# Query features by products of 32 rows with repeated sketch rows, instead of outer products and transposes

## The chip, the cores and the metric

The kernel runs on one core of a Trainium2 chip. The metric is the device time of one execution in microseconds (us); less is better. The core has TensorE (matrix products, "PE" in the profile, with its weight loads listed apart as "PEld"), VectorE (DVE), ScalarE (ACT), GpSimd (POOL) and SyncE (SP), which here only issues transfers. Each engine works through its own list of instructions in order.

## What is computed

Polynomial-sketch attention, followed by a feed-forward layer with a squared ReLU. There are 4 batches with 4 heads of 1088 tokens, of 32 numbers each; the sketches S1 and S2 are 8 x 32; the feed-forward layer takes 4352 tokens of 128 numbers through 2048 and back.

```python
def phi(x):                                   # 32 numbers -> 64 features
    a = np.einsum('rd,bhsd->bhsr', S1, x)
    b = np.einsum('rd,bhsd->bhsr', S2, x)
    return np.einsum('bhsi,bhsj->bhsij', a, b).reshape(*x.shape[:-1], r * r)
q_p, k_p = (phi(q), phi(k))
kv = np.einsum('bhsf,bhsd->bhfd', k_p, v)
z = np.sum(k_p, axis=2)
num = np.einsum('bhsf,bhfd->bhsd', q_p, kv)
den = np.einsum('bhsf,bhf->bhs', q_p, z)[..., None] + 1e-06
x = (num / den), heads side by side           # 4352 x 128
h = np.maximum(x @ w_in, 0.0)
out = h * h @ w_out
```

All inputs and the output are float32.

## The kernel before

**Tiles.** Of each batch's 1088 tokens, 1024 are the main part; the other 64 ("remainder") go through the same steps in small tiles. The main part of a batch b is worked in two halves g, of 512 tokens and 4 heads each. Within a half there are four token tiles t of 128 tokens. The half's attention output, transposed (`xT`, 128 x 512, float16), is a *chunk* of the feed-forward layer. The first half of batch 0 is made in two chunks of 256 tokens, to start early; the remainders are a chunk of 256; that makes ten chunks.

**The feed-forward stream.** For every chunk, `block()` is called once for each of the 16 slices of 128 of the inner 2048 (once for two slices where a chunk has 256 tokens). It multiplies `xT` with a slice of `w_in` in float16 (L763, into `pg` in PSUM), ScalarE takes the ReLU (L770, `gt`), VectorE squares it (L771, `g2`), and TensorE multiplies the square with a slice of `w_o` in float32 (L790, accumulated in `po`). The first product runs about three blocks ahead of the second (`LOOK = 3`). The last chunk's second product has its operands swapped (L800). Results are transposed back (L709), scaled (L738) and stored.

**The attention work** for the next chunks is written as Python generators (`k_gen`, `phi_gen`, `x_gen`, `qrem_phi_gen` and others) that `pump` advances between blocks. A scheduler orders the instructions that this gives on each engine; only `start()`, which brings up the first chunks, is ordered by hand. A PSUM pool with the tag `ms` has two buffers of 128 x 512 float32; the transposes, the projections and the return transposes of the stores take turns on it.

**Features before.** A half of q is first laid out as `xt`, 128 x 512: partition 32 t + d holds number d of token tile t, and the 4 heads with 128 tokens each lie along the free axis. TensorE transposes do it (L235) for the halves (0,0), (0,1) and (3,1), a VectorE transpose of 32 x 32 blocks (L252) for the others. Then:

1. `projected` (L214): TensorE multiplies `xt` with the block matrix `w_bd` into `ab_ps` (128 tokens x 16 sketch values for each head and tile). These are small float32 products: for a half, 16 of them with 32 output rows and 64 columns each (at the start, 8 with 64 output rows). A float32 product is two records in the trace.
2. ScalarE copies `ab_ps` to `ab` (L63).
3. `outer_of` (L256): the 8 x 8 outer products, two instructions of 128 x 512 for a half, on GpSimd for the halves of batches 1 to 3, on VectorE for those of batch 0.
4. The features have to be turned to lie on the partitions, `phT`. For the halves (0,0), (0,1) and (1,0) TensorE transposes them (L437, L396, eight products of 128 x 128 each) and ScalarE copies the result (two copies of 512). For the other five halves `features_by_dma` has ScalarE split the words in 16-bit halves (L416, four copies of 512), stores them in DRAM (L422) and reads them back transposed by a DMA (L425).

With `phT` and the batch's `kvbd` (made from k and v, L318), `numerators` (L214, tile `nd`) gives the numerators and denominators; `normalize` (L478 to L517) divides and scales, and a transpose of `xs` gives `xT`.

k goes through steps 1 to 3 too, and needs no step 4.

Of the kernel before, what the change touches and what calls it, by code (L numbers as in the profile page):

```python
# [9 lines left out]
F16 = mybir.dt.float16  # L10
U16 = mybir.dt.uint16

# [10 lines left out]
def kernel(  # L23
# [29 lines left out]
    fpool = ctx.enter_context(tc.tile_pool(name="ffn", bufs=3))  # L53
    dram = ctx.enter_context(
        tc.tile_pool(name="dram", bufs=2, space=bass.MemoryType.DRAM)
    )
    pspool = ctx.enter_context(
# [119 lines left out]
    nc.scalar.activation(warm[:, 1:2], warm[:, 0:1], Relu)  # L177
    w_bd = cpool.tile([128, H * 16], F32)
    nc.vector.memset(w_bd[:], 0.0)
    kvbd = [cpool.tile([128, 4 * VW], F32, name=f"kvbd{i}") for i in range(2)]  # L180
# [81 lines left out]

    def proj(xt, T, tag, eng, outer, ps_tag="ms", m=32, only=None):

        return features(projected(xt, T, ps_tag, m), T, tag, eng, outer, only)

# [6 lines left out]

    def features(ab_ps, T, tag, eng, outer, only=None):
        ab = apool.tile([128, 256], F32, tag="ab", bufs=3)
        if T == 4:
            evict(
                eng,
                _v(ab, 0, [[16, 4], [64, 4], [1, 16]]),
                _v(ab_ps, 0, [[64, 4], [16, 4], [1, 16]]),  # L280
            )
        else:
            evict(eng, ab[:, 0:64], ab_ps[:, 0:64])
        ph = apool.tile([128, 1024], F32, tag=tag, bufs=3)
        for t0 in range(0, T, 2) if only is None else only:
            outer_of(ab, ph, t0, outer[(t0 // 2) % len(outer)], min(2, T - t0))
        return ph if only is None else (ab, ph)

# [115 lines left out]

    def features_by_dma(ph, eng):

        parted = apool.tile([128, 2048], U16, name="parted", tag="parted")  # L410
        halves = ph.bitcast(U16)

        for x in range(2):
            for y in range(2):
                with tc.issue_after(last_relu[0]):
                    eng.copy(  # L416
                        parted[:, 1024 * x + 512 * y : 1024 * x + 512 * y + 512],
                        _v(halves, 1024 * y + x, [[2, 512]]),
                    )
            yield 1  # L420
        rows_of = dram.tile([128, 2048], U16, name="rows_of", tag="rows_of")
        pinned(nc.sync.dma_start(rows_of[:, :], parted[:, :]))  # L422
        yield 2
        sb = apool.tile([128, 1024], F32, name="phT_d", tag="phT_d")
        pinned(nc.sync.dma_start_transpose(  # L425
            _v(sb.bitcast(U16), 0, [[256, 8], [1, 256]]),
            bass.AP(rows_of.tensor, rows_of.offset, [[1024, 256], [1, 1024]]),
        ))
        yield 4
        return sb  # L430

    def half_features_t(ph, t0, eng):

        t_ps = pspool.tile([128, 512], F32, name="t_ps", tag="ms", bufs=2)
        for pr in range(2):
            for t in range(2):
                nc.tensor.transpose(  # L437
                    t_ps[:, 256 * pr + 128 * t : 256 * pr + 128 * t + 128],
                    ph[:, 256 * (t0 + t) + 128 * pr : 256 * (t0 + t) + 128 * pr + 128],
                    iden[:, :],  # L440
                )
        sb = apool.tile([128, 512], F32, name="phT_h", tag=f"phT{t0 // 2}")
        evict(eng, sb[:, :], t_ps[:, :])
        return [sb[:, 256 * pr : 256 * pr + 256] for pr in range(2)]

    def numerators(b, phT, m, T=4, tag="nd", bufs=1):
        nd = pspool.tile([128, 256 * T], F32, name="nd", tag=tag, bufs=bufs)
        for t in range(T):
            for pr in range(2):
                both = not isinstance(phT, list)  # L450
                tiled(
                    nd, 256 * t + 2 * VW * pr, 2 * VW,
                    phT if both else phT[pr], 256 * t + 128 * pr if both else 128 * t,
                    kvbd[b % 2][:, 2 * VW * pr : 2 * VW * pr + 2 * VW],
                    m=m,
                )
        return nd
# [84 lines left out]
    summed = {0}  # L542
    ab_second = []
    BY_PE = ((0, 1), (B - 1, 1))
# [17 lines left out]
    def half_gen(phT, t0, m, tag, bufs):  # L562

        nd = numerators(0, phT, m, 2, tag, bufs)
        yield 1
# [21 lines left out]

    def phi_gen(b, g, outer):
        eng = nc.scalar
        xt = proj_t(q_sb[b], g, 4, eng) if (b, g) in BY_PE else turned(q_sb[b], g)  # L590
        yield 1
        ph = proj(xt, 4, "ph_q", eng, outer)
        if (b, g) == (1, 0):
            yield 3
            phT = []
            for pr in range(2):
                phT.append(feature_t(ph, 4, pr, eng))
                yield 1
            phT_of[b, g] = phT
            return  # L600
        yield 4
        phT_of[b, g] = yield from features_by_dma(ph, eng)

    def second_gen(outer, m):

        ph = features(ab_second[0], 4, "ph_q", nc.scalar, outer)
        yield 3
        phT = []
        for pr in range(2):
            phT.append(feature_t(ph, 4, pr, nc.scalar))  # L610
            yield 1
        yield from x_gen(0, 1, phT)
# [211 lines left out]
    def start():  # L824
# [3 lines left out]
        for h in range(H):  # L828
            nc.vector.tensor_copy(
                out=_v(w_bd, 16 * h, [[1, 16]], 32 * h, 32),  # L830
                in_=_v(s_ps, 0, [[1, 16]], 32 * h, 32),
            )
        xk.append(proj_t(k_sb[0], 1, 4, act))
        pk = [proj(x, 4, "ph_k", e, (dve,), "pg", m=64) for x, e in zip(xk, (dve, act))]
# [3 lines left out]
        kv0.tiles(pk[0], 0, range(2))  # L838
        pq = proj(xq, 4, "ph_q", act, (dve,), "pg", m=64, only=(0,))
        ph_krem[0] = proj(xkr, 1, "ph_kr", act, (dve,), "pg", m=64)  # L840
        outer_of(*pq, 2, dve)
        kv0.tiles(pk[0], 0, range(2, 4))
        kv0.tiles(pk[1], 1, range(4))
        pqT = [half_features_t(pq[1], 0, act)]
        kv0.finish((dve,))
        half = [half_gen(pqT[0], 0, 64, "pg", 2)]
        next(half[0])

# [7 lines left out]
        for _ in range(3):  # L856
            next(half[0])
        pqT.append(half_features_t(pq[1], 2, act))
        half.append(half_gen(pqT[1], 2, 64, "nd", 1))
        next(half[1])  # L860
# [4 lines left out]
        def rest():  # L865
            yield from half[1]
            yield from second_gen((dve,), 64)

# [5 lines left out]

        return rest(), last_casts(), xq

    second, last_casts, xq = start()
    by_hand.close()
    ab_second.append(projected(xq, 4, "ms", 64))

    for b in range(B):
# [8 lines left out]
        if b + 1 < B:  # L890
            add_work(
                phi_gen(b + 1, 0, (pool,)), phi_gen(b + 1, 1, (pool,)),
                after=7 if b == 0 else 1,
# [60 lines left out]
```

## Time and profile before

| | before |
|---|---|
| median of 3 runs | 208.66 us (208.07 to 208.98) |
| the profiled execution | 208.12 us |
| its span in the profile | 206.2 us |
| granted TensorE clock | 1.00 |
| TensorE busy | 196.8 us, 95% |
| weight loads | 120.1 us, 58% |
| VectorE busy | 146.7 us, 71% |
| ScalarE busy | 112.3 us, 54% |
| GpSimd busy | 45.5 us, 22% |
| outer products of 128 x 512 on GpSimd, half of them q's (L256) | 24, mean 1310 ns |
| the 16-bit copies (L416) | 20, mean 622 ns |
| squares (L771) | 136, mean 778 ns |

"Busy" is the time in which at least one instruction of the engine was running. TensorE's instructions overlap each other, so that a record's own duration is longer than the time by which it holds up the next one; the distance from start to start is what counts. The chain of waits follows the last instruction back to what released it, step by step.

### The profile page before, as it was taken

The page shows a single profiled execution, that of the slowest core. Times are in us where ns is not written, and L with a number is a line of the kernel's source. Part 1 is how long each engine was busy: PE and PEld are TensorE (multiplying, and loading weights), DVE is VectorE, ACT ScalarE, POOL GpSimd, SP SyncE. Part 2 cuts the span into 40 slices and gives each one's busy share as a digit, 9 for nine tenths or more (in the row PEclk, how much of TensorE's full clock was granted, in tenths as well). Part 3 has the DMA queues.
Part 4 walks back from the last instruction along what each step waited for, and adds up shares of the span by engine and source line. Part 5 has one row for each costly group of instructions (what it writes and reads, how often), then busy time and mean ns, then how long its engine had stood idle before and what let it go on. Part 6 is the DMA issues. An engine that isn't in the chain of part 4 may idle for free.

```text
span 206.2 us, 5349 instructions
## 1 busy us (share of the span) xinstructions
PE 196.8 (95%) x2177; PEld 120.1 (58%) x2177; DVE 146.7 (71%) x281; ACT 112.3 (54%) x216; POOL 45.5 (22%) x66
## 2 busy tenths in 40 slices
PE   7979999698999999999999999999999999999993
PEld 6857888474434543554344645455444454779992
DVE  2769769539786799869966896569666887766651
ACT  3548765208755448336755365547755545655540
POOL 1000539242100097105400295114000210000000
PEclk9999999999999999999999999999999999999999
DMA  6899301412468124651260022401440101010001
GB/s 167 218 327 320 70 3 53 111 30 32 116 191 191 30 38 115 136 153 27 61 187 8 17 67 105 102 3 37 150 93 3 51 0 25 5 51 13 16 0 51
DMA packets 40120, 17.39 MB, mean 84 GB/s; under 512 B 27040, under 2 KB 39072, under 8 KB 40096
## 3 DMA queue, kind: packets, MB, share of 16 engines
q1 hardware_dynamic: 40016, 17.05, 31.5%
q8 instruction: 17, 0.28, 0.5%
q14 instruction: 7, 0.06, 0.1%
q10 hardware_dynamic: 80, 0.01, 0.0%
HBM read 8.79 MB, written 4.85 MB: 66 GB/s over the span
## 4 chain that ended last, share of the span: by engine, by line
PE 75%; DVE 9%; POOL 4%; DMA 3%; ACT 3%; issue 3%; SPq 1%; DVEq 0%; ACTq 0%
PE po L790 40%; PE pg L763 12%; PE po L800 7%; POOL ph L256 4%; PE nd L214 4%; PE ab_ps L214 3%; DVE g L771 3%; PE xt_ps L235 2%; DMA t<-in_q_dram 2%; PE kv_first L193 1%; DMA rows_of<-parted 1%; PE kv_ps L318 1%; ACT gt L770 1%; SPq L425 1%; PE kv_first L318 1%
## 5 line engine op out<-in xcount | busy, mean ns | idle before, releaser
L771 DVE TENSOR_TENSOR g<-gt 128x512 f32<-128x512 f32 x136 | 104.0, 778 | 36.9 <-ACT gt L770 36.6
L790 PE MATMUL po<-g,w_o 128*128 128x512 f32 (+1 forms) x288 | 123.8, 526 | 0.4
L770 ACT ACTIVATE gt<-pg 128x512 f32<-128x512 f32 x136 | 81.0, 600 | 50.0 <-PE pg L763 49.0
L790 PEld LDWEIGHTS po<-g,w_o 128*128 128x128 f32 x288 | 52.5, 191 | 26.4 <-issue 12.3
L763 PE MATMUL pg<-xT,w_in 128*128 128x512 f16 x112 | 42.6, 381 | 0.5 <-ACT gt L770 0.4
L256 POOL TENSOR_TENSOR ph<-ab 128x512 f32<-128x512 f32 (+1 forms) x27 | 33.1, 1250 | 17.9 <-ACT ab L63 17.7
L763 PEld LDWEIGHTS <-w_in 128*128 128x128 f16 x160 | 15.3, 98 | 22.3 <-issue 18.7
L514 POOL TENSOR_SCALAR mp<-mm 128x4 f32<-128x4 f32 (+2 forms) x11 | 4.0, 364 | 96.6 <-DVE mm L494 96.6
L800 PEld LDWEIGHTS po<-w_o,g 128*128 128x128 f32 x128 | 16.4, 192 | 0.6
L800 PE MATMUL po<-w_o,g 128*128 128x128 f32 x128 | 16.5, 275 | 0.0
L63 ACT COPY ab<-ab_ps 128x256 f32<-128x256 f32 (+1 forms) x19 | 6.4, 341 | 16.6 <-PE ab_ps L214 16.5
L214 PEld LDWEIGHTS ab_ps<-w_bd,xt 128*32 128x32 f32 (+1 forms) x476 | 8.7, 113 | 7.8 <-ACT gt L770 2.3
L416 ACT COPY parted<-ph 128x512 uint16<-128x512 uint16 x20 | 11.6, 622 | 1.1 <-POOL ph L256 1.1
L214 PE MATMUL ab_ps<-w_bd,xt 128*32 128x64 f32 (+1 forms) x476 | 11.6, 223 | 0.2
L252 DVE STREAM_TRANSPOSE xt<-t 128x512 f32<-128x512 f32 x9 | 6.1, 696 | 3.0 <-DMA t<-in_q_dram 3.0
L63 ACT COPY xt<-xt_ps 128x512 f32<-128x512 f32 (+1 forms) x11 | 5.1, 471 | 4.5 <-PE xt_ps L235 4.4
L318 PEld LDWEIGHTS kv_ps<-v_main,ph 128*32 128x32 f32 x384 | 4.1, 110 | 6.0 <-issue 4.3
L318 PE MATMUL kv_ps<-v_main,ph 128*32 128x33 f32 x384 | 4.9, 198 | 2.0 <-DVE xs L508 1.4
L214 PEld LDWEIGHTS nd<-kvbd,phT_d 128*32 128x32 f32 x320 | 4.9, 110 | 3.2 <-issue 1.7
L63 ACT COPY sb<-t_ps 128x512 f32<-128x512 f32 (+1 forms) x8 | 3.4, 429 | 5.0 <-PE t_ps L396 4.9
L508 DVE TENSOR_TENSOR xs<-nd,small 128x512 f16<-128x512 f32 (+1 forms) x9 | 5.7, 632 | 0.3
L763 PE MATMUL pg<-xT_h,w_in 128*128 128x256 f16 x32 | 5.8, 273 | 0.0
(74 smaller groups left out, 118.1 us busy)
## 6 DMA issues: line engine op xcount, KB each, us to landing
rows_of<-parted SPq DMA_DIRECT2D x5, 512.0 KB, 2.8
t<-in_k_dram SPq DMA_DIRECT2D x3, 512.0 KB, 4.2
t<-in_q_dram SPq DMA_DIRECT2D x3, 512.0 KB, 4.2
out_dram<-o_sb SPq DMA_DIRECT2D x20, 64.0 KB, 1.8
w_in<-in_moe_w_in_dram SPq DMA_DIRECT2D x2, 512.0 KB, 7.6
w_o<-in_moe_w_out_dram SPq DMA_DIRECT2D x2, 512.0 KB, 8.5
v_turned<-in_v_dram SPq DMA_DIRECT2D x64, 16.0 KB, 2.0
k_sb<-in_k_dram SPq DMA_DIRECT2D x2, 256.0 KB, 3.0
```

The costliest lines, as they stand in the source:

```text
L63: return nc.scalar.copy(dst, src)
L214: nc.tensor.matmul(out_ps[p0 + c : p0 + c + m, c0 : c0 + w], lhsT[:, l0 + c : l0 + c + m], rhs,)
L252: nc.vector.transpose(out=xt[:, :], in_=_v(src, 128 * g, [[NJ * D, 4], [1, 128]]))
L256: eng.tensor_tensor(out=_v(ph, 256 * t0, [[64, 4 * w], [8, 8], [1, 8]]), in0=_v(ab, 64 * t0, [[16, 4 * w], [1, 8], [0, 8]]), in1=_v(ab, 64 ...
L318: nc.tensor.matmul(self.ps[c : c + self.m, at : at + w], _v(ph, c0 + 128 * pr + c, [[1, self.m]], p0, n), v_of(2 * pr + c // 64), start=c ...
L416: eng.copy(parted[:, 1024 * x + 512 * y : 1024 * x + 512 * y + 512], _v(halves, 1024 * y + x, [[2, 512]]),)
L508: nc.vector.tensor_tensor(out=_v(xs, 0, [[128, T], [32, 4], [1, 32]]), in0=num, in1=_v(rs, 0, [[4, T], [1, 4], [0, 32]]), op=mult,)
L763: nc.tensor.matmul(pg[:, nt * i : nt * i + nt], w_in[:, 128 * (c + i) : 128 * (c + i) + 128], xT[:, 0:nt],)
L770: last_relu[0] = nc.scalar.activation(gt[:, :], pg[:, :], Relu).ins
L771: nc.vector.tensor_tensor(out=g2[:, :], in0=gt[:, :], in1=gt[:, :], op=mult)
L790: last_product[0] = nc.tensor.matmul(po[0][:, 0:nt], w_o[:, 128 * c : 128 * c + 128], g2[:, nt * i : nt * i + nt], start=(c == 0), stop=(c ...
L800: nc.tensor.matmul(po[t // 2][:, 128 * (t % 2) : 128 * (t % 2) + 128], g2[:, 128 * t : 128 * t + 128], w_o[:, 128 * c : 128 * c + 128], st ...
```

## The change

Features of q are made in their final layout at once. In `start()`, two copies make `w_rep`, 128 x 128: on each group of 32 partitions, the columns 0 to 63 are the rows of S1, each repeated 8 times in a row, and the columns 64 to 127 the rows of S2, all 8 repeated 8 times over. `features_direct` then multiplies, for a token tile t, its 32 partitions of `w_rep` with its 32 partitions of `xt`: 64 features come out on 64 partitions, for two heads side by side (c = 0, 1), once for the factor a and once for the factor b. ScalarE copies the a part from PSUM (`a_rep`), and VectorE multiplies it with the b part, straight into `phT`.

A half takes two calls of `features_direct`, with two tiles t each. A call has 8 float32 products with 32 contraction rows, 64 output rows and 256 columns, 2 copies of 128 x 256 and 2 multiplications of 128 x 256. It takes both buffers of the tag `ms`, one for each t. Gone for q's main halves are `projected`, its copy, the outer products, the transposes of features, the 16-bit copies and the ten transfers through DRAM. k and the remainders keep the old way. In the changed program the halves (2,0) and (3,0) have their first call taken apart by the scheduler: the four products of one t, a first product of the feed-forward stream, then the four of the other t.

```diff
+    w_rep = cpool.tile([128, 128], F32)
...
-    def features_by_dma(ph, eng):
...
-        for x in range(2):
-            for y in range(2):
-                with tc.issue_after(last_relu[0]):
-                    eng.copy(
-                        parted[:, 1024 * x + 512 * y : 1024 * x + 512 * y + 512],
-                        _v(halves, 1024 * y + x, [[2, 512]]),
+    def features_direct(xt, ts, phT):
+        f = {t: pspool.tile([128, 512], F32, name="f_ps", tag="ms", bufs=2) for t in ts}
+        for ab in range(2):
+            for t in ts:
+                for c in range(2):
+                    nc.tensor.matmul(
+                        f[t][64 * c : 64 * c + 64, 256 * ab : 256 * ab + 256],
+                        w_rep[32 * t : 32 * t + 32, 64 * ab : 64 * ab + 64],
+                        _v(xt, 128 * c, [[256, 2], [1, 128]], 32 * t, 32),
                     )
...
-        pinned(nc.sync.dma_start(rows_of[:, :], parted[:, :]))
...
-        pinned(nc.sync.dma_start_transpose(
...
+        a = apool.tile([128, 512], F32, name="a_rep", tag="a_rep", bufs=3)
+        for i, t in enumerate(ts):
+            nc.scalar.copy(a[:, 256 * i : 256 * i + 256], f[t][:, 0:256])
+        for i, t in enumerate(ts):
+            nc.vector.tensor_tensor(
+                out=phT[:, 256 * t : 256 * t + 256],
+                in0=a[:, 256 * i : 256 * i + 256], in1=f[t][:, 256:512], op=mult,
+            )
...
-    def phi_gen(b, g, outer):
+    def phi_gen(b, g):
         eng = nc.scalar
         xt = proj_t(q_sb[b], g, 4, eng) if (b, g) in BY_PE else turned(q_sb[b], g)
         yield 1
-        ph = proj(xt, 4, "ph_q", eng, outer)
...
+        phT = phT_tile()
+        for x in range(2):
+            features_direct(xt, (2 * x, 2 * x + 1), phT)
+            yield 1
+        phT_of[b, g] = phT
...
+        nc.vector.tensor_copy(
+            out=_v(w_rep, 0, [[8, 8], [1, 8]]), in_=_v(s_ps, 0, [[1, 8], [0, 8]])
+        )
+        nc.vector.tensor_copy(
+            out=_v(w_rep, 64, [[8, 8], [1, 8]]), in_=_v(s_ps, 8, [[0, 8], [1, 8]])
+        )
...
         kv0.tiles(pk[0], 0, range(2))
-        pq = proj(xq, 4, "ph_q", act, (dve,), "pg", m=64, only=(0,))
         ph_krem[0] = proj(xkr, 1, "ph_kr", act, (dve,), "pg", m=64)
-        outer_of(*pq, 2, dve)
         kv0.tiles(pk[0], 0, range(2, 4))
+        phT = phT_tile()
+        features_direct(xq, (0, 1), phT)
         kv0.tiles(pk[1], 1, range(4))
-        pqT = [half_features_t(pq[1], 0, act)]
         kv0.finish((dve,))
-        half = [half_gen(pqT[0], 0, 64, "pg", 2)]
+        features_direct(xq, (2, 3), phT)
+        half = [half_gen(phT, 0, 64, "pg", 2)]
```

## The prediction

> **What bounds the kernel.** I read the engines' shares first, then the chain of waits, then TensorE's order of time, then its idle time by stage.
>
> ```profile
> PE 196.8 (95%) x2177; PEld 120.1 (58%) x2177; DVE 146.7 (71%) x281; ACT 112.3 (54%) x216; POOL 45.5 (22%) x66
> ```
>
> A busy share alone proves nothing, since records overlap. The chain of waits, in a stretch without attention work, does:
>
> ```profile
> 63.45 0.22 PE pg L763
> 63.67 0.86 PE po L790 x2
> 64.53 0.22 PE pg L763
> 64.75 0.86 PE po L790 x2
> ...
> 192.42 0.89 PE po L800 x8
> ```
>
> A block lasts 1.08 us, and all of it is TensorE: 0.22 for one float16 product of 512 columns and 0.86 for one float32 product, two records of 0.43. In the same block ScalarE works 0.60 and VectorE 0.69, so both have slack. The price goes with the columns: a record of 512 columns takes 0.43, one of 128 columns 0.89/8 = 0.11 us. A record of 256 columns thus takes 0.215.
>
> Where attention work is put between blocks, it lengthens TensorE's list (order of time):
>
> ```profile
> 115.87 0.60 PE L709 MATMUL o_ps<-iden,oT 128*128 128x128 f32 x4
> ...
> 116.40 0.65 PE L214 MATMUL ab_ps<-w_bd,xt 128*32 128x64 f32 x32
> ...
> 116.99 0.39 PE L763 MATMUL pg<-xT,w_in 128*128 128x512 f16 x1
> ```
>
> The projection of a half, 32 records, holds TensorE from 116.40 to 116.99, 0.59 us. A record of 64 columns should take 0.055; 32 one after another would take 1.8. So four run side by side, each on 32 output columns of the array: 8 x 0.055 = 0.45. The remaining 0.14, and 0.09 more by which the four transposes before took longer than 4 x 0.11, is the change to narrow products and back. I call that 0.24 us for a group.
>
> The stages show how much waiting there is to win (columns are the stage, its length, then each engine's busy time):
>
> ```profile
> 2.00:17.00 15.00, 13.53 (x207) 10.96 (x208) 8.96 (x31) 7.53 (x17) 0.85 (x4) 1.00 0.98 281
> 17.00:30.00 13.00, 12.91 (x143) 10.60 (x140) 9.96 (x16) 10.05 (x22) 3.74 (x5) 1.00 0.43 112
> 30.00:50.00 20.00, 17.43 (x408) 12.96 (x406) 13.15 (x28) 7.96 (x17) 9.56 (x12) 1.00 0.25 57
> 68.00:100.00 32.00, 31.59 (x487) 15.49 (x486) 27.27 (x52) 17.01 (x35) 14.34 (x17) 1.00 0.35 79
> 113.00:136.00 23.00, 22.91 (x431) 12.32 (x433) 16.19 (x27) 12.73 (x27) 9.44 (x9) 1.00 0.24 65
> ```
>
> TensorE idles 2.6 us at 30 to 50 and hardly anywhere after it. Distances from start to start, against the prices above, add a little: 3.3 us of waits at 30 to 50, 1.4 at 68 to 100, 0.5 at 17 to 30, 1.7 at the start.
>
> **Removed from TensorE.** I count seven halves, all but (0,0), which is at the start. Each loses a projection, 0.45 + 0.24 = 0.69: 4.8 us. Halves (0,1) and (1,0) lose 8 transposes each: 16 x 0.11 = 1.8. Sum 6.6. The other five halves were transposed by DMA, off TensorE, so nothing else comes back there.
>
> **Added to TensorE.** A call of `features_direct` is 8 products, 16 records of 256 columns, each on 32 rows and 64 columns of the array. Four different tiles follow each other (two t, two c). No row shows products side by side on different rows. Bounds: four side by side, as the projection has it by columns, 16 x 0.215/4 = 0.86; two by two, 1.72; one by one, 3.44. With 0.24 that is 1.10, 1.96 or 3.68. I take 1.10: the projection is the nearest row, and each t has its own PSUM buffer. 14 calls make 15.4 us. In the changed program's order two calls stand in two halves, one t each; a half has two tiles only and lasts 8 x 0.215/2 + 0.24 = 1.10, so each costs a call more: 2.2. Five calls have a third product of the first t ahead of the second t's, on a tile in use: 0 to 2 records each, I take one, 0.2: 1.0. Sum 18.6, net +12.0 us.
>
> The Trainium skill ("TensorE: Matmul & The Clock Gate", Part 3, "Measured speedup vs the span model") reports 3.07 times, not 4, for four products of 32 rows side by side. An estimate by it makes a call 16 x 0.215/3.07 + 0.24 = 1.36, and the sum 16 x 0.26 = 4.2 us higher.
>
> **The start.** There the chain decides. Before, the first half's normalization begins at 13.07 on VectorE; its four small transposes and copy (10.82 to 12.1) go. In their place two calls stand among the k products, and the second call's two multiplications stand ahead of that normalization on VectorE. They wait for a call that ends near 12.6, so it begins near 13.7: +0.6 us (0 to 1.5). Two copies for `w_rep` (near 0.3 each, like the 0.295 us copy of `kvbd`) fall where VectorE waits for `ab_ps`.
>
> **The other engines.**
>
> ```profile
> L256 POOL TENSOR_TENSOR ph<-ab 128x512 f32<-128x512 f32 x24 | 30.8, 1310 | 11.9 <-ACT ab L63 11.7
> ...
> L416 ACT COPY parted<-ph 128x512 uint16<-128x512 uint16 x20 | 11.6, 622 | 1.1 <-POOL ph L256 1.1
> ...
> L63 ACT COPY ab<-ab_ps 128x256 f32<-128x256 f32 x15 | 5.6, 373 | 15.1 <-PE ab_ps L214 15.1
> ...
> L738 DVE TENSOR_TENSOR o_sb<-o_ps,beta 128x256 f32<-128x256 f32 x2 | 0.8, 410 | 0.0
> ```
>
> These are groups of instructions (busy time, mean ns of one, idle time before). The single line on the squares adds least, median and longest:
>
> ```profile
> L771 DVE TENSOR_TENSOR g<-gt x136: 627/693/1551, 17.1 to 199.7; 128x512 f32<-128x512 f32 x136
> ```
>
> VectorE gains 32 multiplications, priced by the 410 ns row: +13.1, and loses four outer products of 0.69: -2.7. Squares have a median of 693 but a mean of 778 ns, and the long ones lie beside GpSimd's outer products (at 118 to 122 us one of 1.10 and two that make 2.64). Half of those outer products go, so perhaps half of 136 x 0.085 = 11.6 us. VectorE ends near 151 us: not a bound. ScalarE loses 20 x 0.62, 8 x 0.37 and six copies of 0.58, and gains 32 x 0.37: about -7 us, hidden. GpSimd loses 12 x 1.31. The ten DRAM transfers free SP's queue, where the load of q at 86.9 stands behind one of them; TensorE is full there.
>
> **Waits.** *Won:* at 36 us TensorE waits 1.4 us for k's products, as GpSimd has a queue of six outer products, and again 0.6 at 40.7. Only k's stay, so I take 2.4 of the 3.3 us there, and 0.6 of the 1.4 at 68 to 100, where squares come late beside GpSimd: -3.0 (0 to -6.9, with all waits listed). *New:* a call holds both `ms` buffers until VectorE has multiplied. A second call follows a block later, 1.08 us; copy, multiplication, and a ReLU or square in front of each take up to 0.37 + 0.41 + 0.60 + 0.69 = 2.1. Behind it on TensorE the next block's products are queued. Bounds 0 and 14 x 1.2 = 17. The copy of a needs the first half of a call only, and existing waits of this kind are under 0.8, so I take near the lower end, 0.27 for each of seven second calls: +1.9.
>
> Sum: 12.0 + 0.6 - 3.0 + 1.9 = +11.5 us on the profiled 208.12 (span 206.2 and 1.9 around it). The median is 0.54 higher: 208.66 + 11.5 = 220.2 us.
>
> **Rivals.** *Two by two:* the rows of the array do not run side by side. A call takes 1.96: 14 x 1.96 + 2 x 0.24 - 6.6 = +21.3; the start +2, waits -3 + 1: 230.0 us. For: no row shows it otherwise. Against: nothing in the column case hints at it. The Trainium skill (same page and part, "The mechanism") says that a weight load overlaps a running product only where their row groups differ. By that rule c = 0 and c = 1 of one t would follow each other, which gives this rival's time. The trace disagrees for columns: the projection's loads all use 128 rows, and 32 of them fit in its 0.59 us.
>
> *The buffers:* waits for `ms` reach 1.0 us a call, 14 us instead of 1.9: 232 us. For: VectorE's list mixes normalization (3 us for a half) with the multiplications. Against: where VectorE is as full before, at 68 to 100 us, TensorE still waits only 1.4 us.
>
> *Faster:* the columns of a 32-row product stream twice as fast, the two records of a product running together. A call is 0.43 + 0.24 = 0.67, sixteen (with split ones) 10.7 - 6.6 = 4.1, and all 6.9 us of waits go, with 0.3 at the start: 206.2 us. It decides from a call below 0.82 us, with all waits won. Against: at 128 rows a column costs the same for 128, 256 and 512 columns, and the waits would all have to go at once.
>
> **Numbers.** My forecast 0.67, two by two 0.16, the buffers 0.08, faster 0.06, one by one 0.03 (14 x 1.72 above two by two, 254 us). My forecast's own range, from its bounds, is 213.5 to 226 us. To hold 8 in 10 the range takes in two by two: 212.5 to 231.5. About 0.5% is what a measurement of this kernel can tell from no change. Faster by more 0.06, within it 0.02, slower 0.92.
>
> **What would show it.** Groups of 16 records of `f_ps`, 1.1 us from the first start to the next product; starts four together, 0.215 apart. TensorE at 95% or more, its list 12 us longer, GpSimd near 25 us, ScalarE near 105. No gap at 36 us. The forecast is wrong if a call takes 1.9 us, if TensorE stands idle before `f_ps` for over 5 us in all, or if the span is under 211.

## The result, and the profile after

The changed kernel takes 225.46 us (median of 6 runs, 225.2 to 226.9), the kernel before beside it 208.82: a ratio of 1.0805, with a 95% interval of 1.0763 to 1.0847. A second series of the same two kernels gave 1.0691 (1.0638 to 1.0745). The forecast was 220.2 us, slower by 11.5; measured were 16.6 and, in the second series, 14.4 (0.0691 x 207.81). That second ratio rests on two of its four runs (222.15 and 222.78 us); the other two (226.31 and 226.49 us, at mean clocks of 0.977 and 0.976) lie over 1.5% above them and are left out, although two runs of the first series took as long at the same clocks (225.88 and 226.9 us).

The engines' shares of the changed kernel, from its page:

```profile
PE 213.4 (96%) x2185; PEld 126.3 (57%) x2185; DVE 145.8 (65%) x311; ACT 108.9 (49%) x214; POOL 28.0 (13%) x54
```

TensorE is the bound as before, with 16.6 us more of busy time. VectorE, ScalarE and GpSimd have less to do. The groups (busy time, mean ns of one, idle time before):

```profile
L743 DVE TENSOR_TENSOR g<-gt 128x512 f32<-128x512 f32 x136 | 94.7, 702 | 37.9 <-ACT gt L742 36.1
...
L421 DVE TENSOR_TENSOR phT_q<-a_rep,f_ps 128x256 f32<-128x256 f32 x32 | 12.5, 418 | 16.7 <-ACT a_rep L419 16.7
L412 PE MATMUL f_ps<-xt,w_rep 32*64 32x256 f32 x256 | 23.0, 388 | 0.0
L419 ACT COPY a_rep<-f_ps 128x256 f32<-128x256 f32 x32 | 11.1, 374 | 20.0 <-PE f_ps L412 19.8
L254 POOL TENSOR_TENSOR ph<-ab 128x512 f32<-128x512 f32 (+1 forms) x15 | 15.1, 1024 | 37.2 <-ACT ab L59 37.2
```

The new multiplications cost VectorE 12.5 us. They are paid for by four outer products that go (2.7 us) and by the squares, whose mean falls from 778 to 702 ns. In the profile before, the 20 squares that overlap an outer product of GpSimd last 1.27 us on average and the others 0.69; after, 9 overlap one, and they last 0.74, which the smaller number of outer products alone does not explain. L412 is what TensorE got for it: 256 records.

The timeline shows how long a call of `features_direct` holds TensorE (start, duration, count; in brackets the idle time before and its releaser):

```profile
27.42 1.09 PE L412 MATMUL f_ps<-xt,w_rep 32*64 32x256 f32 x16
28.44 0.39 PE L735 MATMUL pg<-xT_h,w_in 128*128 128x256 f16 x2
...
80.35 1.08 PE L412 MATMUL f_ps<-xt,w_rep 32*64 32x256 f32 x8
81.36 1.12 PE L762 MATMUL po<-g,w_o 128*128 128x512 f32 x2
...
82.42 0.65 PE L212 MATMUL ab_ps<-w_bd,xt 128*32 128x64 f32 x32
...
83.00 1.70 PE L412 MATMUL f_ps<-xt,w_rep 32*64 32x256 f32 x16
...
83.19 0.37 ACT L59 COPY ab<-ab_ps 128x256 f32<-128x256 f32 x1 [1.34 <-PE ab_ps L212]
...
84.63 0.39 PE L735 MATMUL pg<-xT,w_in 128*128 128x512 f16 x1
```

A whole call lasts 1.02 us from its start to the next product (27.42 to 28.44), its 16 records in four groups of four. Half a call, with one t, lasts 1.01 (80.35 to 81.36): with two tiles of the array instead of four, half the work takes the same time. The call at 83.00 takes 1.63: one of the two `ms` buffers still holds the `ab_ps` of 82.42, which ScalarE copies until 83.56, so one t goes two by two first and the other follows. Five of the whole calls are of this kind. All calls together hold TensorE 21.8 us.

Two stretches hold what the forecast did not have. The first is the start, in stages (length, busy time of PE, PEld, DVE, ACT, POOL, granted clock, DMA share, GB/s):

```profile
13.00:17.00 4.00, 3.32 (x74) 2.38 (x70) 2.41 (x9) 1.80 (x5) 0.00 (x0) 1.00 1.09 367
17.00:23.00 6.00, 4.26 (x19) 3.15 (x20) 5.48 (x16) 3.54 (x7) 2.71 (x7) 0.72 0.90 229
```

```profile
18.10 0.28 PE L513 MATMUL x_ps<-iden,xs 128*128 128x128 f16 x2 [1.48 <-DVE xs L489]
...
20.93 2.54 PE L762 MATMUL po<-g,w_o 128*128 128x256 f32 x6
```

TensorE waits for `xs`, the granted clock falls to a mean of 0.72, and six records of 256 columns take 2.54 us, against 1.56 in e12, where the clock stays at 1.00. The second is the load of q for batch 2. SP's own queue, before and then after:

```profile
33.55 0.36 SPq L746 DMA_DIRECT2D out_dram<-o_sb  x1
...
53.42 0.39 SPq L83 DMA_DIRECT2D t<-in_q_dram  x1
```

```profile
42.23 0.37 SPq L718 DMA_DIRECT2D out_dram<-o_sb  x1
42.69 1.18 SPq L79 DMA_DIRECT2D t<-in_k_dram  x1
43.93 16.95 SPq L110 DMA_DIRECT2D v_turned<-in_v_dram  x32
60.98 0.39 SPq L79 DMA_DIRECT2D t<-in_q_dram  x1
```

and what comes of it on TensorE and VectorE:

```profile
41.21 0.38 PE L681 MATMUL o_ps<-iden,oT 128*128 128x128 f32 x2
...
64.31 0.38 PE L735 MATMUL pg<-xT,w_in 128*128 128x512 f16 x1
65.11 0.71 DVE L250 STREAM_TRANSPOSE xt<-t 128x512 f32<-128x512 f32 x1 [3.62 <-DMA t<-in_q_dram]
65.74 0.65 DVE L743 TENSOR_TENSOR g<-gt 128x512 f32<-128x512 f32 x1
...
66.45 1.12 PE L762 MATMUL po<-g,w_o 128*128 128x512 f32 x2 [1.76 <-DVE g L743]
```

The order on SP is that of before: the first output store, then k, 32 transfers of v, then q. But the store needs the return transposes `o_ps`, which take turns on `ms`, and these now stand behind the calls of (0,1) and (1,0) on TensorE's list. They start at 41.21 instead of 31.85 us, the store at 42.23 instead of 33.55, and q's load at 60.98 instead of 53.42. A transpose of that q stands ahead of a square on VectorE, so VectorE waits 3.62 us (1.32 before) and TensorE waits for the square, which it did not before.

By chunks (the start of each chunk's first product with `w_o`, before and after, in these two profiles) the 17.2 us by which the span grew come as follows: the start +3.1, chunk 0 to 1 +5.2, 1 to 2 -2.5, 2 to 3 +1.7 (the late q), 3 to 4 +5.0, 4 to 5 -0.3, 5 to 6 +5.1, and -0.1 in all that follows.

### The profile page after: what moved, and what is told of

It is laid out like the page before. It is cut to its first block, busy times and chain, and to the rows that moved or that the text cites. A ratio compares the mean times of both kernels' runs of the same rounds, so it can differ in the third digit from the quotient of the medians.

```text
span 223.4 us, 5360 instructions
## 1 busy us (share of the span) xinstructions
PE 213.4 (96%) x2185; PEld 126.3 (57%) x2185; DVE 145.8 (65%) x311; ACT 108.9 (49%) x214; POOL 28.0 (13%) x54
## 4 chain that ended last, share of the span: by engine, by line
PE 88%; DMA 6%; DVE 3%; ACT 1%; issue 0%; SPq 0%; DVEq 0%; ACTq 0%
PE po L762 44%; PE pg L735 14%; PE f_ps L412 10%; PE po L772 6%; PE nd L212 4%; DMA t<-in_q_dram 4%; PE ab_ps L212 3%; PE xt_ps L233 3%; PE kv_ps L316 2%; DMA k_sb<-in_k_dram 2%; PE o_ps L681 1%; PE kv_first L316 1%; DVE xt L250 1%; ACT xt L59 1%; DVE phT_q L421 1%; DVE g L743 1%
## 5 line engine op out<-in xcount | busy, mean ns | idle before, releaser
L743 DVE TENSOR_TENSOR g<-gt 128x512 f32<-128x512 f32 x136 | 94.7, 702 | 37.9 <-ACT gt L742 36.1
L421 DVE TENSOR_TENSOR phT_q<-a_rep,f_ps 128x256 f32<-128x256 f32 x32 | 12.5, 418 | 16.7 <-ACT a_rep L419 16.7
L412 PE MATMUL f_ps<-xt,w_rep 32*64 32x256 f32 x256 | 23.0, 388 | 0.0
L419 ACT COPY a_rep<-f_ps 128x256 f32<-128x256 f32 x32 | 11.1, 374 | 20.0 <-PE f_ps L412 19.8
L254 POOL TENSOR_TENSOR ph<-ab 128x512 f32<-128x512 f32 (+1 forms) x15 | 15.1, 1024 | 37.2 <-ACT ab L59 37.2
L412 PEld LDWEIGHTS f_ps<-xt,w_rep 32*64 32x64 f32 x256 | 11.7, 131 | 7.5 <-DVE phT_q L421 2.2
L212 PEld LDWEIGHTS nd<-kvbd,phT_q 128*32 128x32 f32 (+1 forms) x480 | 8.0, 111 | 5.3 <-PE pg L735 2.6
L212 PE MATMUL nd<-kvbd,phT_q 128*32 128x66 f32 (+1 forms) x480 | 9.4, 222 | 0.3 <-DVE phT_q L421 0.3
L212 PEld LDWEIGHTS ab_ps<-w_bd,xt 128*32 128x32 f32 (+1 forms) x252 | 5.4, 124 | 5.6 <-ACT gt L742 1.5
L212 PE MATMUL ab_ps<-w_bd,xt 128*32 128x64 f32 (+1 forms) x252 | 7.2, 235 | 0.1
```

The lines of the kernel that those rows point to most:

```text
L212: nc.tensor.matmul(out_ps[p0 + c : p0 + c + m, c0 : c0 + w], lhsT[:, l0 + c : l0 + c + m], rhs,)
L254: eng.tensor_tensor(out=_v(ph, 256 * t0, [[64, 4 * w], [8, 8], [1, 8]]), in0=_v(ab, 64 * t0, [[16, 4 * w], [1, 8], [0, 8]]), in1=_v(ab, 64 ...
L412: nc.tensor.matmul(f[t][64 * c : 64 * c + 64, 256 * ab : 256 * ab + 256], w_rep[32 * t : 32 * t + 32, 64 * ab : 64 * ab + 64], _v(xt, 128 ...
L419: nc.scalar.copy(a[:, 256 * i : 256 * i + 256], f[t][:, 0:256])
L421: nc.vector.tensor_tensor(out=phT[:, 256 * t : 256 * t + 256], in0=a[:, 256 * i : 256 * i + 256], in1=f[t][:, 256:512], op=mult,)
L743: nc.vector.tensor_tensor(out=g2[:, :], in0=gt[:, :], in1=gt[:, :], op=mult)
```

## The experiments

Lines of their code have other numbers than in the kernels shown. "Edit" is against the changed kernel unless said otherwise.

**e1: the start as before.** Edit: `start()` makes the half (0,0) with outer products and transposes again.

```diff
+        pq = proj(xq, 4, "ph_q", act, (dve,), "pg", m=64, only=(0,))
...
+        outer_of(*pq, 2, dve)
...
-        features_direct(xq, (0, 1), phT)
...
+        pqT = [half_features_t(pq[1], 0, act)]
...
-        features_direct(xq, (2, 3), phT)
```

> The changed kernel, but the first half (0,0) in start() is made the old way (projection, outer products on VectorE, eight TensorE transposes); all other halves stay with features_direct. Theory 'the start': the first block came 3.0 us later, and TensorE's long wait before it (1.65 us at 16.4) brings down its clock, so that records of 0.216 take 0.43 us until 22.9; both go. Expected 225.5 - 3.0 - 1.5 = 221.0 us. Rival 'the start is cheap': it costs 0.6 us as predicted and the rest of the 3.0 us is k's transfer, which landed 0.75 us later in that one execution: 224.9 us, with the clock still low.

Measured: 223.21 us (220.85 to 224.16), ratio 1.0707 (1.0636 to 1.0777). The start's loss went, with the first chunk 0.2 us after that of before, but the late q took most of it back (TensorE's timeline):

```profile
60.44 0.38 PE L751 MATMUL pg<-xT,w_in 128*128 128x512 f16 x1
64.07 2.04 PE L778 MATMUL po<-g,w_o 128*128 128x512 f32 x2 [3.25 <-DVE g L759]
```

The wait became 3.25 us, and the two records after it took 2.04 instead of 1.02 us. The step from chunk 2 to 3 is +4.7 us, against +1.7 and +2.5 in the two profiles of the changed kernel: TensorE's list reaches the squares earlier, and q still comes behind 17 us of v's transfers. One of the four runs kept a mean clock of 1.00 and took 220.85 us; the three at 0.990 and 0.991, the profiled one among them, took 222.61 to 224.16.

**e4: q's load ahead of v's.** Edit: the load of q for batch 2 is issued before those of k and v.

```diff
+            q_sb[b + 2] = load(q, b + 2, "q_sb", True)
             if b == 0:
                 k_sb[b + 2] = load(k, b + 2, "k_sb", True)
                 v_sb[b + 2] = load_v(b + 2)
-            q_sb[b + 2] = load(q, b + 2, "q_sb", True)
```

> The changed kernel with the load of q for batch 2 issued ahead of batch 2's k and v (of which v is 32 transfers on SP's queue). Theory 'late q': VectorE waits 3.6 us for q at 61 to 65 us with two squares behind it, and TensorE waits 1.9 us for the squares; that goes: 223.6 us, and no wait over 0.7 us in 54 to 75. Rival 'moved': v's features come late instead, or the scheduler puts other work there, 225.5 us.

Measured: 220.81 us (220.46 to 221.24), ratio 1.0609 (1.0580 to 1.0639). The wait is gone, the step from chunk 2 to 3 is -0.5 instead of +1.7 us, and the result is better than expected. The runs also lie closer together.

**e3: the order within a call.** Edit: the loops over the factor and over t swapped, and the order kept by hand.

```diff
-        for ab in range(2):
-            for t in ts:
+        for t in ts:
+            for ab in range(2):
```

> The changed kernel with the same 8 products in each call, but all four of one token tile ahead of the four of the other, and kept in that order. Theory 'four tiles side by side, in order': only two tiles (c = 0, 1) can run at once, so a call goes from 1.03 us to 16 x 0.215/2 = 1.7, start to next product. Against the calls of the changed kernel's trace (21.3 us with the changes of form for the seven halves) 14 calls of 1.96 make 27.4, and the two at the start 0.7 more each: 225.5 + 6.1 + 1.4 = 233 us. Rival 'order does not matter': TensorE takes the free tile whatever the order, 225.5 us.

Measured: 224.8 and 226.5 us in the two runs that can be compared, against 225.5 for the changed kernel, which is no difference that they can tell. The calls last as long as before, here one whole call and half of one:

```profile
25.38 1.11 PE L414 MATMUL f_ps<-xt,w_rep 32*64 32x256 f32 x16
26.42 0.39 PE L739 MATMUL pg<-xT_h,w_in 128*128 128x256 f16 x2
...
79.91 1.08 PE L414 MATMUL f_ps<-xt,w_rep 32*64 32x256 f32 x8
80.92 1.12 PE L766 MATMUL po<-g,w_o 128*128 128x512 f32 x2
```

A whole call starts four records within 34 ns, although the program now has all four products of one t ahead of those of the other (the trace does not say which tile each record is on). So the order of the products in a call is not what costs.

**e5: four token tiles in a call.** Edit: a half in one call of 16 products, two t in the buffers of `ms`, two in the buffer of the numerators (tag `nd`).

```diff
-        for x in range(2):
-            features_direct(xt, (2 * x, 2 * x + 1), phT)
-            yield 1
+        features_direct(xt, (0, 1, 2, 3), phT)
+        yield 2
...
+            wide = pspool.tile([128, 1024], F32, name="f_nd", tag="nd", bufs=1)
```

> The changed kernel, but the halves after the start have all four token tiles in one call, with 16 products: t = 0, 1 in the ms buffers, t = 2, 3 in the two banks of the nd tile; products go a of all tiles, then b, kept in order. Theory 'every tile of the array at once': eight products (four t, two c) side by side, so a half takes 32 x 0.215/8 + 0.24 = 1.10 us instead of two calls; five halves are still parted by the scheduler, some 0.8 us each: 12 us for the seven halves against 21.3, 216.5 us. Rival 'four at most': 32 x 0.215/4 + 0.24 = 1.96 a half, 18 us in all, 222 us.

Measured: 218.06 us (217.52 to 218.59), ratio 1.0476 (1.0440 to 1.0512). One whole call on TensorE's timeline:

```profile
26.67 0.45 PE L418 MATMUL f_ps<-xt,w_rep 32*64 32x256 f32 x4
26.70 0.45 PE L418 MATMUL f_nd<-xt,w_rep 32*64 32x256 f32 x4
...
27.37 0.39 PE L418 MATMUL f_ps<-xt,w_rep 32*64 32x256 f32 x4
27.40 0.39 PE L418 MATMUL f_nd<-xt,w_rep 32*64 32x256 f32 x4
27.72 0.39 PE L742 MATMUL pg<-xT_h,w_in 128*128 128x256 f16 x2
```

32 records take 1.05 us (26.67 to 27.72), eight starting together: twice the work in the time of a call with two t. What kept the gain below the full one is that the scheduler took five of the halves apart, and that the late q was still there.

**e6: the changed kernel again**, unedited.

> The changed kernel itself, beside the next three on the same chip. If its first block comes at 18.8 us again (before: 15.9), the late start of its first profile is the kernel's own; the four kernels with the same start had 17.3, and then 1.4 us of the 3.0 belong to the change and the rest to that execution. Expected 225 us, first block near 17.3.

Measured: 222.15 and 222.78 us in the two runs behind the ratio of 1.0691, 226.31 and 226.49 in the others, as told above. In its profile the start costs +1.2 us instead of +3.1. Of the 1.9 between, 1.5 lie ahead of the change: in the first profile TensorE begins k's transposes at 4.66 us, having waited for `k_sb`, and the first q transposes at 8.85; here it does so at 4.06 and 7.35, with the same instructions up to there. The late k is 0.6 of it, and the rest is the pace. In the first microseconds of the profiles before, after, e6 and e12 TensorE's records are about twice as far apart as later: transposes of 128 columns start 0.215 us apart instead of 0.11. That ends near 5.4 us here and near 4.1 us in e12; in the first profile it covers the whole projection of k too, which holds TensorE 1.91 us (6.94 to 8.85) instead of 1.08 (6.27 to 7.35). The profile's rows give the granted clock as 1.00 all the while, so the mean clock of a run does not show it.

**e9: the start's second multiplications later.** Edit, against e4: the two multiplications of the second call are issued behind the first half's normalization.

```diff
-        features_direct(xq, (2, 3), phT)
+        held = features_direct(xq, (2, 3), phT, True)
...
+        multiply(*held, (2, 3), phT)
```

> The changed kernel with q's early load (as in the run with that name) and one more edit: in the start, the two multiplications of the second call stand behind the first half's normalization on VectorE, not ahead of it. Theory 'order on VectorE': the normalization waits for the second call and its multiplications; freed of them the first block comes 0.8 to 1.0 us earlier, TensorE's wait of 1.65 us before it shrinks, and if that wait is what brings the clock down, the low clock after it goes too: 220.8 - 1.0 - 1.2 = 218.6 us. Rival 'second half is next': the second half's chunk then comes late by as much and the blocks wait there, 220.8 us.

Measured: 221.38 us (221.29 to 221.6), ratio 1.0641 (1.0605 to 1.0676): no gain. TensorE's list has the second half's `nd` ahead of the first half's transposes, and that `nd` now waits:

```profile
16.14 1.15 PE L212 MATMUL nd<-kvbd,phT_q 128*64 128x66 f32 x16 [2.45 <-DVE phT_q L426]
17.23 0.40 PE L518 MATMUL x_ps<-iden,xs 128*128 128x128 f16 x2
```

The work was moved out of the way on one engine and stood in the way on the next.

**e7: the wide call everywhere.** Edit: as e5, with the tiles of `nd` first and the calls kept whole, q loaded early as in e4, the late multiplications of e9, and one wide call in the start too.

> All halves, the start's too, with four token tiles in one call of 16 products, t = 2, 3 in the banks of nd and their products first, which leaves every call whole in the program's order; q's load early; in the start the multiplications of t = 2, 3 behind the first normalization. Theory 'every tile at once': a half costs TensorE 1.05 + 0.1 instead of 2.1 to 3.5 us: against the run with four at once 13.1 - 7.4 us of calls go, 1.4 us of waits behind split calls, 2.1 us of late q, and 1.5 to 2.5 us at the start: 207 us, level with the kernel before. Rival 'nd is in the way': the nd banks are held by features until VectorE has multiplied, numerators and k's sums wait for them, and TensorE idles instead, 212 us.

Measured: 211.01 us (210.86 to 212.08), ratio 1.0152 (1.0118 to 1.0186). All calls together hold TensorE 9.8 us instead of 21.8, and the middle of the kernel is about 1 us behind that of before. The rest is the start:

```profile
15.92 1.15 PE L212 MATMUL nd<-kvbd,phT_q 128*64 128x66 f32 x16 [2.87 <-DVE phT_q L437]
```

**e11: e7 with the old start.**

> As e7 (every half in calls of 16 products, q loaded early), but the half (0,0) made the old way, with outer products and transposes. Theory (the start, with its wait of 3.0 us at 12.8 and the low clock behind it, is 2.2 to 2.7 of the 3.2 us by which e7 is slower): about 208.5 us, level with before. Rival (the start's loss is made up of something that another wait takes over later, as the late q did in e1): 211 us.

Measured: 208.61 us (207.27 to 210.26), ratio 1.0019 (0.9992 to 1.0046). With the start as before and wide calls for the other seven halves the change costs nothing that can be told from none.

**e8: two halves only.** Edit, against the kernel before: the halves (0,1) and (1,0), whose features TensorE turned, are made by wide calls; the rest is as before.

```diff
-            phT = []
-            for pr in range(2):
-                phT.append(feature_t(ph, 4, pr, eng))
-                yield 1
+            phT = phT_tile()
+            features_direct(xt, (0, 1, 2, 3), phT)
+            yield 2
```

> The kernel before, with only the halves (0,1) and (1,0) made by the direct products, four token tiles in one call; the start and the other five halves stay as before (outer products on GpSimd, transposes by DMA). Theory 'one part alone': each of the two costs TensorE 1.15 us and saves a projection of 0.69 and transposes of 0.88, and GpSimd's queue at 29 to 36 us is two outer products shorter, so that the waits of 1.4 and 0.6 us for k's features go: 208.2 - 0.8 - 1.5 = 206 us. Rival 'covered': the waits move to VectorE, which has 8 multiplications more there, and nothing is won, 208 us.

Measured: 211.21 us (209.84 to 212.87), ratio 1.0149 (1.0103 to 1.0195): slower. At chunk 3 it is 0.6 us ahead of before; then it loses 3.4. SP's own queue, and TensorE:

```profile
65.20 17.48 SPq L114 DMA_DIRECT2D v_turned<-in_v_dram  x32
...
84.61 0.61 SPq L423 DMA_DIRECT2D rows_of<-parted  x1
...
88.33 1.83 SPq L426 DMA_TRANSPOSE phT_d<-rows_of  x1
...
92.77 1.13 PE L215 MATMUL nd<-kvbd,phT_d 128*32 128x66 f32 x64 [3.18 <-DMA phT_d<-rows_of]
```

The half (2,1) still goes through DRAM, and its store stands on SP behind 32 transfers of v, which take 17.5 us to issue. It does so in the kernel before as well, but there they begin at 61.62 us and the store at 81.21; here both are 3.4 to 3.6 us later.

**e10: e8 with the loads reordered.** Edit, against e8: q ahead of k and v for batch 2, and batch 3's k and v behind its q.

```diff
-        if 0 < b < B - 2:
-            k_sb[b + 2] = load(k, b + 2, "k_sb", True)
-            v_sb[b + 2] = load_v(b + 2)
...
             q_sb[b + 2] = load(q, b + 2, "q_sb", True)
+            k_sb[b + 2] = load(k, b + 2, "k_sb", True)
+            v_sb[b + 2] = load_v(b + 2)
```

> The kernel before with the halves (0,1) and (1,0) alone made directly, each in one call of 16 products (as in e8), and the loads reordered: the load of q for batch b+2 is issued ahead of those of k and v, and batch 3's k and v move from the start of batch 1's loop to its middle, so that the store and the transposing transfer of the half (2,1) are no longer queued behind 32 transfers of v on SP. Theory (e8 loses its gain only to that queue): the wait of 3.3 us at 89 us goes, TensorE's list is shorter by 1.5 to 2 us than before, about 206 us, ratio 0.993. Rival (the list gained nothing, or k and v of batch 3 now come late): 209 to 211 us, with the wait at another place.

Measured: 208.44 us in eleven of twelve runs (207.32 to 209.61; the other took 211.72), ratio 0.9998 (0.9975 to 1.0021). The wait is gone:

```profile
81.11 0.34 SPq L423 DMA_DIRECT2D rows_of<-parted  x1
84.12 1.92 SPq L426 DMA_TRANSPOSE phT_d<-rows_of  x1
...
90.09 1.14 PE L215 MATMUL nd<-kvbd,phT_d 128*32 128x66 f32 x64
```

The store is issued 3.5 us earlier, and `nd` at 90.09 waits for nothing. The queue was the cause of e8's loss, but the gain that I expected over before did not come. From chunk 0 to 1, where the wide call of (0,1) stands, the step is 1.2 us longer than before, and the next two steps win 0.5 and 0.4 back. Most of the 1.2 is work that moved: the numerators of (0,1), 1.1 us of TensorE, stand in this stretch (27.05 us) and stood in the next one before (32.16). TensorE does wait 1.1 us for the borrowed tile of the numerators, but at 33.2 to 34.3 us, ahead of the call of (1,0) and in the next stretch; the expectation of e13 below puts that wait to the call of (0,1).

**e12: TensorE kept busy in the start.** Edit, against e4: three extra products where TensorE waits; nothing uses their result.

```diff
+        busy = pspool.tile([128, 256], F32, name="busy", tag="po", bufs=2)
+        for _ in range(3):
+            nc.tensor.matmul(busy[:, 0:256], zero[:, 0:128], zero[:, 0:256])
         whole(half[0])
```

> As e4 (the changed kernel with q loaded early), with three more float32 products of 256 columns of zeros in the start, 0.43 us each, between the denominators of the first half and the transposes of its x, where TensorE waits 1.65 us; their result is not used. Theory (the wait brings the clock down and so is paid for twice): the granted clock goes from 0.991 to 1.00, the records after it last 0.215 instead of 0.43 us for 256 columns, 1.0 to 1.5 us faster than e4, 219.5 us, ratio 1.055. Rival (the dip has another cause, such as the sparse work before it): the clock stays at 0.991 and the time at 220.8 us.

Measured: 219.75 us (219.4 to 220.04), ratio 1.0549 (1.0520 to 1.0578), against 1.0609 (1.0580 to 1.0639) for e4: 0.6%, some 1.2 us. The stages of e4, then TensorE's timeline and the stages of e12:

```profile
13.00:17.00 4.00, 2.22 (x46) 1.68 (x39) 2.93 (x13) 1.85 (x5) 0.43 (x2) 1.00 1.02 340
17.00:23.00 6.00, 5.71 (x28) 3.94 (x26) 4.42 (x11) 4.72 (x10) 1.52 (x5) 0.72 0.93 262
```

```profile
14.31 1.56 PE L841 MATMUL busy<-zero 128*128 128x256 f32 x6
15.86 0.29 PE L513 MATMUL x_ps<-iden,xs 128*128 128x128 f16 x2
...
18.55 1.56 PE L762 MATMUL po<-g,w_o 128*128 128x256 f32 x6
```

```profile
13.00:17.00 4.00, 3.69 (x44) 2.76 (x39) 3.40 (x16) 2.08 (x6) 0.47 (x3) 1.00 1.07 347
17.00:23.00 6.00, 5.27 (x32) 3.91 (x31) 4.81 (x10) 5.03 (x10) 1.69 (x5) 1.00 0.90 246
```

With the gap filled, the clock stays at 1.00 (0.998 to 1.00 in the four runs, 0.991 to 0.992 in those of e4). More work made the kernel faster, so the wait does bring the clock down. The size is less sure: by chunks 0.6 us of the profiles' difference lies behind the filled gap, while 0.6 lies ahead of it and cannot come from it; the rest comes after chunk 4.

**e13: one half only.** Edit, against e10: (0,1) as before, so that only (1,0) is made by a wide call.

> As e10, but only the half (1,0) made directly, in one call of 16 products; (0,1) keeps its outer products on VectorE and its transposes on TensorE. In e10 the stretch with the call of (0,1) was 1.2 us longer than before, 1.1 of it TensorE waiting at 33 us for the tile of the numerators, which that call borrows. Theory (e10's two halves cancel: (0,1) loses there what (1,0) wins): TensorE's list is 0.43 us shorter (0.69 of projection and 0.88 of transposes against 1.14 for the call), and of the wait of 1.57 us at 36 us for k's outer products about 1 us goes, as (1,0)'s no longer stand among them on GpSimd: about 207.1 us, ratio 0.993. Rival (the call of (1,0) has to wait for the borrowed tile as that of (0,1) did, or the wait at 36 us comes back): level with before, 208 to 209 us.

Measured: 207.43 us (206.66 to 208.65), ratio 0.9971 (0.9947 to 0.9995). Of all versions this is the only one whose interval lies below 1, by 0.3%; one interval of 95% among a dozen that just misses 1 may be chance. It was not won where I expected it. TensorE's wait for k's products is 1.15 us, and 1.40 in the same list of before:

```profile
39.20 0.76 PE L319 MATMUL kv_ps<-v_main,ph 128*32 128x33 f32 x64 [1.15 <-DVE xs L538]
```

That is 0.25 us and not 1; both wait for a normalization on VectorE rather than for GpSimd alone. In the profile the start is 0.4 us later than before, the steps up to chunk 3 then win 1.2 (+0.8, -1.3 and -0.7), and nothing else moves by more than 0.2.

## Why the prediction was right, and where it fell short

**The bound and the sign** held: TensorE's list sets the end, and the other engines' savings are worth nothing on their own.

**The price of a call** held. I argued from column tiles that four tiles would run side by side with different rows too: 0.86 us, and 0.24 for the change of shape, 1.10 in all. Start to next product is 1.02, and entry from the product before adds the rest. The starts come four together, 0.22 apart after a first step of 0.27. *Two by two* (1.96 a call) and *faster* (0.67) are refuted by this, and *the buffers* by the row of L412, which has no idle time before it. The rule of the Trainium skill ("TensorE: Matmul & The Clock Gate", Part 3, "The mechanism") that loads overlap only where row groups differ is not borne out here: e5's eight products start together, two on each row group, and the weight loads of the next eight (26.72 to 26.90 us) lie inside them. The 3.07 times that the same part reports, for four row groups, is not seen either: 16 records in 1.02 us are 3.4 times as fast as 16 x 0.215 one after another with the change of shape in it, and its four groups, 0.22 apart, make it 4 without. The sum by that figure, 220.2 + 4.2 = 224.4 us, lies nearer to the measured time, but by luck: a whole call with both buffers free takes 1.11 us with the entry, not its 1.36.

**The sum of TensorE's list** held between the chunks, and its agreement in total is partly luck. e12, which has neither the late q nor the low clock, is 11.4 us longer than before in its span (217.6 against 206.2), and +11.5 was the forecast. Chunks 0 to 3: +1.2 (4.24 - 2.48 - 0.53), forecast 1.3 by the terms of (0,1), (1,0) and (1,1): 6 x 1.10 + 0.2 + 3 x 0.27 - 3 x 0.69 - 1.8 - 2.4. Chunks 3 to 6: +9.6 (4.95 - 0.48 + 5.08), forecast 9.5 by the terms of the other four: 10 x 1.10 + 0.8 + 4 x 0.27 - 4 x 0.69 - 0.6. The start, +0.7 against 0.6, agrees only in e12. From q's first transposes to the first product with `w_in` it takes 8.54 us before and in e1, which has the old start, but 9.73 in e4 and e6, 9.81 in e12 and 10.00 in the first profile. So the change costs 1.2 to 1.5 us there, and e12 makes up for 0.6 of it by reaching those transposes at 6.80 us instead of 7.36, which is no work of the change.

**The third product of a t** was right in size but not in cause. Five calls are longer, by 0.6 us each; I had charged 0.2 each for a tile in use and 1.9 us for new waits, together 2.9, and 5 x 0.6 = 3.0 was measured. That the two agree is luck. e3 shows that the order does not matter, and the trace shows the reason: one of the two buffers is still held by another tile.

**The waits at 36 us** went, but not for the reason that I gave. I had k's products wait for GpSimd's six outer products. In the profile before, these are done at 36.35 us; TensorE waits on for `xs`, a normalization on VectorE that ends at 37.71. It reads the tile `nd`, and `kv_ps` takes the same buffer next:

```profile
37.85 0.76 PE L318 MATMUL kv_ps<-v_main,ph 128*32 128x33 f32 x64 [1.40 <-DVE xs L508]
```

In the changed kernel `kv_ps` comes at 45.74 us, behind other work, and waits for nothing. GpSimd went to 28.0 us (near 25, though the prediction's own 12 x 1.31 off 45.5 makes 29.8), ScalarE to 108.9 (near 105), VectorE to 145.8 (151, with the squares' gain less than it turned out).

**SP's queue** is the step that failed. I wrote that the ten DRAM transfers free it and that this is worth nothing, as TensorE is full there. I looked only at what leaves the queue and not at the order of what stays: the new calls take the turns on `ms` from the return transposes, those hold up the first output store, and behind the store on SP stand k, v and q. That the turns on `ms` put the return transposes so late is read from the order on TensorE's list and was not tested by itself. The late q was 1.8 and 2.5 us of TensorE's waiting in the two profiles, and e4 takes it away by moving one line: the ratio goes from 1.0691 to 1.0609 (1.0805 in the first series).

**The start** was under-estimated, 0.6 for 1.2 to 1.5 us as told above, and the wait of 1.5 us for `xs` was not in the sum at all as a cause of a lower clock. In the stages that I read of before the clock was 1.00, so I had no term for it. In the first profile the low clock adds about 1.0 us between chunks 0 and 1 (5.22 against 4.24 in e12).

So the first profile's 17.2 us are: the list 11.4, the late q 2.3 (1.7 against -0.5), the low clock 1.0, 2.4 by which its start is later than e12's, and 0.1 elsewhere. Of the 2.4, 2.0 are there at the first transposes of q (8.85 against 6.80 us), ahead of the change's first product: 0.8 is k's load and the rest the slow pace. Why k came late and why the slow pace lasted stays open. This is also the account of one execution: its mean clock was 0.992, that of the other five runs of its series 0.976 to 0.983, so the low clock probably took more of their time, and no trace of them is on record. The forecast's miss is thus 3 to 5 us rather than one figure.

## What to carry to other kernels

A product of few rows and few output columns should share the array with as many others as fit: four products cost the same time as eight here (1.01 and 1.02 us, and sixteen 1.05), so a helper that is called with half of the tiles throws half of the array away, and a scheduler that splits a call in two doubles its price. Where a new step takes turns on a shared buffer, follow what else takes turns there to the end of its chain, transfers in an in-order queue included: the late q (e4) and the late store (e8, e10) were each 2 to 3 us, and each went with a reordered load. A gain in one stretch is kept only if the next wait does not grow by it, so read the start of each stage before and after, not the total alone.

## What the runs showed of the hardware that I had not expected

**Eight products of 32 rows and 64 columns run side by side**, on four row groups and two column groups: 32 float32 records of 256 columns in 1.05 us, where one after another they would take 32 x 0.215 = 6.9.

**A short wait can cost a second time.** In e4 the clock was full until 17 us and half (0.50 and 0.51) from there to about 20.4, after a wait of 1.5 us with little work ahead of it. It depends on more than the length: e8's wait of 3.2 us at 90 us left the clock at 1.00 in its profile, e1's of 3.25 us brought it to 0.53 and 0.61 in the next two stages of 2 us. The Trainium skill ("TensorE: Matmul & The Clock Gate", Part 1) has the gate fall back after an idle window of about 3.4 us. e4's dip began after less than that, so a window that is merely sparse seems to be enough here; where such windows begin, no run here shows.
